# A fused linear-attention and mixture-of-experts kernel: new delays and draws in the order laid out at build time, TensorE by due time, one ones-product for each batch's norm

## The chip, the cores and the metric

The kernel runs on one core of a Trainium2 chip. The metric is the device time of one execution in microseconds. A core has five engines with queues of their own, each worked through in order: TensorE (matrix products, PE in the profile, with its weight loads as PEld), VectorE (DVE), ScalarE (ACT), GpSimd (POOL) and SyncE (SP, which here only issues DMAs). They meet at semaphores. Products land in PSUM, which is eight banks here, called u1, u2, db and ab, two of each; all else lies in SBUF or in DRAM.

## The reference

```python
kv  = einsum('bhsd,bhse->bhde', k, v)            # 8 batches, 8 heads, 576 tokens, 64 wide
o   = einsum('bhsd,bhde->bhse', q, kv)
rms = sqrt(mean(o * o, axis=-1, keepdims=True) + 1e-06)
x   = (o / rms * g_norm) -> (4608, 512)          # tokens by heads*width
p   = domain_probs / (domain_probs.sum(-1) + 1e-09)
for e in range(4):                               # w1[e]: 512x1024, w2[e]: 1024x512
    h = maximum(x @ w1[e], 0)
    out += p[:, e:e+1] * (h @ w2[e])
```

All is float32. The outer loop over experts is 90% and more of the arithmetic.

## The kernel before

**Tiling and steps.** The 4608 tokens are cut into nine chunks of 512: 512 tokens of each of the eight batches, and a ninth chunk with the 64 tokens left of each. The work is 36 steps, step s = 9 e + i, expert e outermost. A step has two parts. `up` makes the hidden layer of a chunk (x w1, then relu), `down` multiplies it with w2, scales it by the probability and adds it to the output, for the first expert by a plain store, for the others by a DMA that adds in DRAM, for the very last step by loading the sum, merging in SBUF and storing. `down` of one step runs beside `up` of the next.

**Fewer products.** Both parts use a scheme with seven products in place of eight, on two levels in `up`: 49 products of 128x128x128 for each of four blocks' worth of work. The operands of the seven are sums and differences of blocks (named 1, 2, 21 or 12, 3 to 7), made on VectorE and GpSimd. In the inner scheme of `up` (lines around 1385 and 1393) and `down_deep` (1707, 1715) ScalarE copies a PSUM bank to another bank as a seed or to SBUF (`snap`), and VectorE adds two of them. `down` has three shapes: seven outer products for each of two token halves, with no inner scheme (the last step); the mixed shape, with outer products 1, 6, 5, 7 plain and 4, 2, 3 by the inner scheme, called from `down` into `down_deep` (steps 0 to 6); and `down_deep` for all seven (steps 7 to 34). One plain product is 16 instructions of 256 columns, one inner product of `up` 8 instructions of 128 columns, one inner product of `down_deep` 16 for a pair of outer forms or 8 for a single one.

**Attention.** `opening` does batch 0 in a way of its own. `attention` does batches 1 to 7, each in the step before the one that needs it, in two halves s of four heads: load q, k, v; transpose q on VectorE (L1023); k times v on TensorE (L1050); q times that (L1075); evacuate four banks, on ScalarE or VectorE (L999, L1000); square on ScalarE (L1099, L1105); sum the squares with a matrix of ones (`total`, L1115 for the 512 tokens, L1121 for the 64 left); root on ScalarE (L1131); inverse and one refining step on VectorE (`invert`, L1137 to L1142); write the 160 columns of 16 partitions to DRAM (`roots`, L1151) and read them back, spread over all partitions (L1158, L1164); scale (L1173, L1180). `x_forms` then makes the seven forms of the chunk and keeps them in DRAM for the later experts.

**The order.** Nothing of the order of instructions is left to run time. Every piece of work is an `Op` given to `Plan.add` with a key (its place in the steps), a cost for each engine that may do it, buffers read and written, and kilobytes if it is a DMA. `Plan.prepare` gives each a due time: the sum of TensorE's costs ahead of its key, then pulled forward along dependencies. `Plan.run` plays the five engines through in time: an engine that is free looks through its pending operations within `REACH` of its first key; SP and TensorE take the first by key that is ready, the others the one with the smallest due time. `ready` says when: after the end of what it depends on plus `CROSS` = 0.2 us, or `SAME` = 0.06 on the same engine; when buffers are free; when one of SP's eight lanes is; and, for operations with `port`, when the port that VectorE and GpSimd share is. `begin` books the times. `deal` adds to the due times of a step a normal draw, whose number for each step is written down in `DEALS`. The order so found is issued as it stands, with waits where the data ask for them. A plan that is wrong about a time thus makes an engine wait on the chip; it doesn't change the order there.

```python
                    best = op
                    if eng in ("PE", "SP"):
                        break
```

Of the kernel before, what the change touches and what calls it, by code (L numbers as in the profile page):

```python
# [42 lines left out]
class Plan:  # L43
# [11 lines left out]
    CROSS, SAME, LANES = 0.2, 0.06, 8  # L55
# [6 lines left out]
    SPREADS = 1.0, 2.0, 4.0  # L62
    DEALS = {
        -2: 25, -1: 39, 0: 49, 1: 28, 2: 72, 3: 8, 5: 18, 6: 22, 7: 12, 8: 22, 9: 17, 10: 9, 11: 22, 12: 28,
        13: 4, 14: 5, 17: 5, 18: 3, 19: 1, 20: 5, 21: 4, 26: 4, 27: 4, 28: 1, 29: 2, 35: 2
# [6 lines left out]
    def add(self, key, cost, fn, reads=(), writes=(), parts=(), kb=0, after=(), port=False, holds=(),  # L72
            early=False, gang=False):
# [3 lines left out]
        op.early, op.gang = early, gang  # L77
# [21 lines left out]
    def prepare(self, slots, later, idle, idle_banks, idle_until):  # L99
# [26 lines left out]
        for op in reversed(self.ops):  # L126
            for d in op.deps:
                cross = self.SAME if op.cost.keys() == d.cost.keys() else self.CROSS
                d.due = min(d.due, op.due - cross - min(d.cost.values()))
# [19 lines left out]
        self.bus, self.port = 3.8, 0.0  # L149
# [10 lines left out]

    def deal(self, step, n):

        draw = random.Random(100 * n + step)
        for op in self.steps[step] + self.steps.get(step + 1, []):
            op.due = op.base + (draw.gauss(0.0, self.SPREADS[n % 3]) if n else 0.0)

# [11 lines left out]
    def save(self):  # L178
        copied = {
            name: {k: type(v)(v) for k, v in getattr(self, name).items()}  # L180
            for name in ("free", "slots", "todo", "waiting", "first")
        }
        copied.update({name: dict(getattr(self, name)) for name in ("live", "ended", "missing", "busy", "written")})
        copied.update({name: list(getattr(self, name)) for name in ("later", "lanes", "wake", "order")})
        copied.update({name: getattr(self, name) for name in ("worked", "bus", "port", "t", "left")})
        return (
            copied, [(o.start, o.end, o.eng) for o in self.ops],
            [(b.left, b.slot, b.ap) for b in self.all_bufs],
        )

    def restore(self, saved):
        copied, ops, bufs = saved
        for name, value in copied.items():
            if isinstance(value, dict):
                value = {k: type(v)(v) if isinstance(v, (dict, list)) else v for k, v in value.items()}
            elif isinstance(value, list):
                value = list(value)
# [177 lines left out]
def kernel(  # L375
# [1194 lines left out]
    def down(s, e, c, mixed=False):  # L1570
# [6 lines left out]
        for t in range(2):  # L1577
# [37 lines left out]
            if mixed:  # L1615
                continue
# [304 lines left out]
```

## Time and profile before

| | |
|---|---|
| median of 3 runs | 1645.11 us (1644.44 to 1647.65) |
| profiled execution | 1645.75 us, span 1644.0 us |
| granted TensorE clock | 1.00 |
| DVE instructions | 2191 |
| DMA | 240.82 MB, 225436 packets |

The span runs from the first to the last instruction of the profiled execution. A matrix product's instructions overlap one another, so the time of a run of them is read from the start of one group to the start of the next, not from a group's busy time. In rows of the timeline the columns are start, length, engine, line, operation, tiles, shape and count, and in brackets the idle time of the engine ahead of it and what ended it. Line 501 is the product of two halves of 64 columns that all parts of the experts use; line 524 is every sum or difference of operands on VectorE and GpSimd; line 530 is every plain load.

### The profile page before, as it was taken

What the parts mean: (1) busy time and instruction counts of PE and PEld (TensorE: products, weight loads), DVE (VectorE), ACT (ScalarE), POOL (GpSimd) and SP (SyncE); (2) the same over time, 40 slices, a digit from 0 to 9 for tenths busy, and PEclk for the clock granted to TensorE, in tenths of its full rate; (3) what the DMA queues carried; (4) which work ended last, traced back from release to release, by engine and by line L of the source; (5) the groups of instructions that cost most, each with busy time, mean ns of one, the idle gap of its engine ahead of it and who ended that gap; (6) DMA issues with size and microseconds to landing.
All of it is one profiled execution on the core that took longest, in us unless ns stands there. A gap on an engine that the chain in (4) does not pass through costs nothing.

```text
span 1644.0 us, 66026 instructions
## 1 busy us (share of the span) xinstructions
PE 1632.1 (99%) x28652; PEld 1551.9 (94%) x28652; DVE 1285.5 (78%) x2191; ACT 972.8 (59%) x2436; POOL 687.0 (42%) x668
## 2 busy tenths in 40 slices
PE   9999999999999999999999999999999999999998
PEld 5588888988999999999999999999999999999996
DVE  5888877788888877877778877777788787677764
ACT  3455554555566666666666666666666566666662
POOL 4232443333433354554354454443455455433331
PEclk9999999999999999999999999999999999999999
DMA  9787786645655435444567454444578444444442
GB/s 237 205 210 185 217 228 174 173 154 187 214 159 152 109 101 149 125 111 111 168 168 162 112 122 111 116 111 115 138 189 184 118 112 117 118 117 106 117 105 52
DMA packets 225436, 240.82 MB, mean 146 GB/s; under 512 B 100954, under 2 KB 165114, under 8 KB 225146
## 3 DMA queue, kind: packets, MB, share of 16 engines
q1 hardware_dynamic: 201594, 199.81, 39.6%
q0 software_dynamic: 23552, 36.78, 14.9%
q8 instruction: 225, 3.69, 0.9%
q14 instruction: 65, 0.53, 0.1%
HBM read 162.21 MB, written 74.33 MB: 144 GB/s over the span
## 4 chain that ended last, share of the span: by engine, by line
PE 97%; DMA 1%; DVE 1%; SPq 0%; issue 0%; ACT 0%; DVEq 0%
PE u L501 48%; PE db L501 31%; PE ab L501 15%; PE ab L1050 1%; DMA kv<-in_v_dram 1%; PE ab L1075 0%; PE ab L1115 0%; DMA big<-in_v_dram 0%; PE db L1075 0%; DMA big<-roots 0%; SPq L530 0%; DVE big L524 0%; DVE big L1173 0%; PE db L902 0%; PE u L863 0%; DMA kv<-in_k_dram 0%
## 5 line engine op out<-in xcount | busy, mean ns | idle before, releaser
L524 DVE TENSOR_TENSOR big<-big,big 128x1024 f32<-128x1024 f32 (+1 forms) x552 | 517.8, 956 | 25.5 <-ACT big L1349 9.8
L501 PE MATMUL u<-xf,big 128*64 128x128 f32 x6496 | 473.6, 273 | 0.0
L501 PE MATMUL db<-big,big 128*64 128x128 f32 (+1 forms) x5328 | 407.5, 292 | 2.0 <-ACT snap L1707 1.2
L501 PE MATMUL u<-xf,w1y 128*64 128x128 f32 x5304 | 396.2, 273 | 0.0
L501 PEld LDWEIGHTS u<-xf,big 128*64 128x64 f32 x6496 | 378.7, 137 | 3.4 <-issue 0.8
L501 PEld LDWEIGHTS db<-big,big 128*64 128x64 f32 x5328 | 316.9, 137 | 29.8 <-ACT snap L1707 1.4
L1393 DVE TENSOR_TENSOR big<-u,snap 128x256 f32<-128x256 f32 x462 | 193.3, 420 | 161.6 <-PE u L501 120.4
L501 PEld LDWEIGHTS u<-xf,w1y 128*64 128x64 f32 x5304 | 310.7, 137 | 3.3 <-issue 1.2
L524 POOL TENSOR_TENSOR big<-big,big 128x256 f32<-128x256 f32 (+1 forms) x169 | 204.4, 1212 | 214.0 <-DVE big L524 89.4
L1385 ACT ACTIVATE snap<-u 128x256 f32<-128x256 f32 x490 | 187.4, 383 | 172.1 <-PE u L501 142.6
L1385 ACT ACTIVATE big<-u 128x256 f32<-128x256 f32 x462 | 175.9, 383 | 76.1 <-PE u L501 52.7
L524 POOL TENSOR_TENSOR big<-big 128x512 f32<-128x512 f32 (+1 forms) x92 | 111.0, 1208 | 161.6 <-DVE big L524 74.5
L1707 ACT ACTIVATE snap<-db 128x256 f32<-128x256 f32 x252 | 89.0, 354 | 128.9 <-PE db L501 116.9
L1349 ACT ACTIVATE big<-big 128x1024 f32<-128x1024 f32 x134 | 140.9, 1051 | 7.8 <-DVE big L524 7.8
L1558 POOL DMA_DIRECT2D out_dram<-big x114 | 99.5, 1122 | 52.2 <-ACT big L1534 43.1
L1715 DVE TENSOR_TENSOR big<-ab,snap 128x256 f32<-128x256 f32 x174 | 73.2, 420 | 59.7 <-ACT snap L1707 39.2
L1385 ACT ACTIVATE u<-u 128x256 f32<-128x256 f32 x245 | 90.8, 371 | 46.9 <-PE u L501 33.3
L524 DVE TENSOR_TENSOR big<-big 128x512 f32<-128x512 f32 (+1 forms) x137 | 102.0, 750 | 1.7 <-POOL big L524 1.1
L1746 POOL TENSOR_TENSOR big<-big 128x512 f32<-128x512 f32 x26 | 33.1, 1274 | 145.9 <-DVE big L524 143.1
L1534 ACT ACTIVATE big<-big,p_all 128x256 f32<-128x256 f32 x190 | 88.8, 500 | 1.8 <-DVE big L1746 1.6
L501 PE MATMUL ab<-kv,big 128*64 128x128 f32 x1296 | 89.8, 273 | 0.0
L501 PE MATMUL ab<-big,big 128*64 128x128 f32 (+1 forms) x1280 | 88.9, 277 | 0.0
(218 smaller groups left out, 2317.2 us busy)
## 6 DMA issues: line engine op xcount, KB each, us to landing
xf<-x SPq DMA_DIRECT2D x104, 512.0 KB, 3.6
xf<-x_h SPq DMA_DIRECT2D x85, 256.0 KB, 3.1
xf<-x SPq DMA_DIRECT2D x78, 256.0 KB, 4.2
out_dram<-big POOLq DMA_DIRECT2D x78, 256.0 KB, 5.9
x<-xf SPq DMA_DIRECT2D x36, 512.0 KB, 3.6
big<-in_moe_w_dram SPq DMA_DIRECT2D x29, 512.0 KB, 6.3
x_h<-big SPq DMA_DIRECT2D x17, 512.0 KB, 3.5
big<-in_moe_w_dram POOLq DMA_DIRECT2D x17, 512.0 KB, 6.1
```

Of the source, the lines that this page charges most:

```text
L501: nc.tensor.matmul(out_[cols], lhsT=lhsT[:, cols], rhs=rhs, **kw)
L524: lambda eng: adder(eng).tensor_tensor(out=out_(), in0=a(), in1=b(), op=op),
L1050: nc.tensor.matmul(bank.ap[o * D:(o + 1) * D, r * D:(r + 1) * D], lhsT=ks[r], rhs=vs[r], start=(j == r == 0), stop=(j == len(sets[0]) - 1) ...
L1349: lambda eng: nc.scalar.activation(out=b.ap[:], in_=b.ap[:], func=ACT.Relu),
L1385: lambda eng: nc.scalar.activation(out=where(), in_=ps.ap[:, 0:HN], func=ACT.Copy),
L1393: lambda eng: nc.vector.tensor_tensor(out=block(whole, a, t), in0=src.ap[:, 0:HN], in1=add_.ap[:], op=ALU.add),
L1534: lambda eng: nc.scalar.activation(out=cell(i, half), in_=ap(), func=ACT.Copy, scale=prob()),
L1558: nc.gpsimd.dma_start(out=dst, in_=cell(i)[parts, :], accum_op=ALU.add)
L1707: lambda eng: nc.scalar.activation(out=where(), in_=group_of(ps.ap), func=ACT.Copy),
L1715: lambda eng: nc.vector.tensor_tensor(out=cell(tq, dq), in0=group_of(src.ap), in1=group_of(add_.ap), op=ALU.add,),
L1746: lambda eng: adder(eng).tensor_tensor(out=whole(to), in0=whole(a), in1=whole(b), op=ALU.add),
```

## The change

It has four parts.

1. The plan's picture of time. One delay across engines becomes several: after TensorE 0.25, to TensorE 0.06, to GpSimd 0.16, on the same engine 0.07, otherwise 0.05, after a landing 0.1, and a buffer is free 0.25 after TensorE or 0.08 after others. An engine may start its next operation before the last ends (`OVERLAP`). The shared port costs -0.14 or 0.1 when it changes hands (`TURN`). The DMAs have a landing time of their own kind, and the rate of the bus is 260 from 45 us on. Some costs of operations change.
2. The choice. TensorE no longer takes the first by key that is ready but the smallest due time, as VectorE, ScalarE and GpSimd do; only SP keeps to the key. The draws are made by a hash, TensorE's with spreads of their own, and `DEALS` has other numbers. To keep the plan legal, the first product of a bank in `up_plain` is named as a dependency of the others.
3. Attention. Evacuations are all on ScalarE. The sums of squares of both halves are one product over 2 x (8 x 4 + 4) calls of 32 columns into one bank of 128 columns, with one root and one inversion for a batch. The result is written in four DMAs (two for each half, 64 partitions, 128 bytes each) and spread as before, the main part now from one run of 1024 values for each half of the partitions.
4. The end. The last two chunks of the last expert change places (8, then 7). The last step uses the mixed shape, with forms 4, 2, 3 ahead in key order, the plain 1, 6, 5, 7 behind, no dependency between the two, banks u1 for its second and third sums, and stores after the plain ones. Of the last expert's inner w2 operands only those of 1, 6, 5, 7 get a buffer apart.

```diff
-    CROSS, SAME, LANES = 0.2, 0.06, 8
+    LANES = 8
+    AFTER_PE, TO_PE, TO_POOL, SAME, OTHER, LANDED, FREED = 0.25, 0.06, 0.16, 0.07, 0.05, 0.1, 0.08
+    OVERLAP = {"PE": 0.0, "DVE": 0.085, "ACT": 0.105, "POOL": 0.05, "SP": 0.0}
+    TURN = {"DVE": -0.14, "POOL": 0.1}
...
+    SPREADS_PE = 0.0, 0.5, 1.5
+    RATE, OPEN = 260.0, 45.0
+    FIRST = "SP",
     DEALS = {
...
     def deal(self, step, n):
 
-        draw = random.Random(100 * n + step)
+        k = len(self.SPREADS)
+        wide = self.SPREADS[n % k] if n else 0.0
+        wide_pe = self.SPREADS_PE[n // k % len(self.SPREADS_PE)] if n else 0.0
         for op in self.steps[step] + self.steps.get(step + 1, []):
-            op.due = op.base + (draw.gauss(0.0, self.SPREADS[n % 3]) if n else 0.0)
+            z = wide_pe if "PE" in op.cost else wide
+            op.due = op.base + (z * self.noise(n, step, op.n) if z else 0.0)
...
+    def delay(self, d, eng):
+
+        if d.kb:
+            return self.LANDED
+        if d.eng == "PE":
+            return 0.0 if eng == "PE" else self.AFTER_PE
+        if d.eng == eng:
+            return self.SAME
+        return {"PE": self.TO_PE, "POOL": self.TO_POOL}.get(eng, self.OTHER)
...
-            when = max(when, d.end + (self.SAME if d.eng == eng else self.CROSS))
+            when = max(when, d.end + self.delay(d, eng))
...
-            when = max(when, self.port)
+            when = max(when, self.port + (0.0 if eng == self.held else self.TURN[eng]))
...
-                    if eng in ("PE", "SP"):
+                    if eng in self.FIRST:
                         break
...
-            self.bus = max(self.bus, t + 1.5) + op.kb / 215.0
+            self.bus = max(self.bus, t + 1.5) + op.kb / (215.0 if t < self.OPEN else self.RATE)
             op.end = self.bus + 0.5
+            if t >= self.OPEN:
+                op.end = max(op.end, t + op.lands)
             self.lanes = self.lanes[1:] + [op.end]
         else:
-            op.end = self.busy[eng] = t + op.cost[eng]
+            op.end = t + op.cost[eng]
+            self.busy[eng] = op.end - self.OVERLAP[eng]
             if op.kb:
-                op.end += 9.0 if op.kb == 512 else 8.0
+                op.end += op.lands
...
-    sides = const.tile([P, 48], F32, name="sides")
-    ones = [sides[:, 16:48], sides[:, 0:32]]
+    sides = const.tile([P, 60], F32, name="sides")
+    ones = [sides[:, 28 - 4 * i:60 - 4 * i] for i in range(8)]
...
-            def total(eng, ss=ss, xh=xh, s=s):
-                for o in range(2):
+        when = at(3.7)
+        ss, wide, both = Buf("ab", f"ss{b}"), 4 * R, x_halves(b)
+
+        def total(eng):
+            for s in range(2):
+                for i in range(8):
                     for j in range(NR):
                         nc.tensor.matmul(
-                            ss.ap[j * R:(j + 1) * R, 0:P], lhsT=ones[o],
-                            rhs=xh.ap[:, (2 * j + o) * P:(2 * j + o + 1) * P],
-                            start=(o == 0), stop=(o == 1), skip_group_check=True,
+                            ss.ap[j * R:(j + 1) * R, 2 * s * R:(2 * s + 1) * R], lhsT=ones[i],
+                            rhs=both[s].ap[:, (8 * j + i) * R:(8 * j + i + 1) * R],
+                            start=(s == i == 0), stop=(i == 7), skip_group_check=True,
                         )
                 for j in range(NR):
                     nc.tensor.matmul(
-                        ss.ap[j * R:(j + 1) * R, P:P + GR], lhsT=ones[0],
-                        rhs=xs.ap[:, s * P + j * GR:s * P + (j + 1) * GR],
+                        ss.ap[j * R:(j + 1) * R, (2 * s + 1) * R:(2 * s + 2) * R], lhsT=ones[0],
+                        rhs=xs.ap[:, s * P + j * R:s * P + (j + 1) * R],
                         start=False, stop=True, skip_group_check=True,
                     )
 
-            plan.add(
-                when, {"PE": 0.75}, total, reads=[xh, xs], writes=[ss]).wide = {ss: P + GR}
+        plan.add(
+            when, {"PE": 1.27}, total, reads=both + [xs], writes=[ss]).wide = {ss: wide}
...
+            for to, src, at_ in (
+                (sent, main[:].rearrange("r (n t) -> n r t", t=R), 2 * s * R),
+                (sent_left, rest_at[:], (2 * s + 1) * R),
+            ):
+                plan.add(
+                    when, SPC,
+                    lambda eng, to=src, at_=at_: nc.sync.dma_start(
+                        out=to, in_=both[0].ap[0:P:2, at_:at_ + R]),
+                    reads=both[:1], writes=[to], kb=8, lands=2.6,
+                )
...
+        ends = s == E * NCH - 1
         order = [m for m in MERGED if not (mixed and m in (2, 4, 3))]
+        if ends:
+            down_deep(s, e, c, ((4, 2), (3,)), base - 0.1, h, merge, send, True)
+            base += 3 / 7
...
-                    after=(second[-1:] if m in (1, 5) else []) + firsts[t:t + 1],
+                    after=(second[-1:] if m in (1, 5) and not ends else []) + firsts[t:t + 1],
...
+    CHUNKS[E - 1][-2:] = NCH - 1, NCH - 2
...
-                down(s, e, c, s < NCH - 2)
+                down(s, e, c, True)
```

231 lines of the change are left out of this document (117 added, 114 removed).

## The prediction

> **What bounds the kernel now.** I read the page first, then the stages, the waits of TensorE, and the timeline at the places where it waits.
>
> ```profile
> span 1644.0 us, 66026 instructions
> PE 1632.1 (99%) x28652; PEld 1551.9 (94%) x28652; DVE 1285.5 (78%) x2191; ACT 972.8 (59%) x2436; POOL 687.0 (42%) x668
> PE 97%; DMA 1%; DVE 1%; SPq 0%; issue 0%; ACT 0%; DVEq 0%
> ```
>
> TensorE is busy for 99% of the span and is 97% of the chain that ended last. The next view cuts the span into stages (busy time of TensorE, of its weight loads, of VectorE, ScalarE and GpSimd, then granted clock and DMA).
>
> ```profile
> 0.00:20.00 20.00, 17.53 (x354) 14.71 (x356) 6.65 (x24) 9.63 (x28) 4.77 (x15) 1.00 0.90 298
> ...
> 840.00:1240.00 400.00, 400.00 (x7334) 400.00 (x7332) 319.95 (x510) 252.39 (x636) 185.16 (x179) 1.00 0.53 133
> 1600.00:1644.00 44.00, 39.10 (x494) 30.47 (x490) 21.99 (x36) 12.85 (x30) 4.78 (x5) 1.00 0.27 49
> ```
>
> The middle, 840 to 1240 us, has no idle time at full clock: an order of the same products can't be shorter there, only longer. Idle time lies in the opening, at the end, and in a few single waits between. The waits of TensorE (total, times, longest):
>
> ```profile
> PE ab L1866 <- POOL ident masks.py:199: 1.4, 1, 1.4
> PE db L501 <- ACT snap L1707: 1.2, 1, 1.2
> PE u L501 <- DVE big L1173: 0.9, 1, 0.9
> PE ab L922 <- DVE big L797: 0.7, 1, 0.7
> PE ab L1050 <- DMA kv<-in_v_dram: 0.6, 1, 0.6
> PE db L501 <- DVE big L1715: 0.6, 1, 0.6
> PE u L501 <- DVE big L1393: 0.5, 1, 0.5
> PE db L501 <- ACT small L1000: 0.5, 1, 0.5
> PE u L863 <- DMA big<-in_v_dram: 0.4, 1, 0.4
> PE db L501 <- ACT big L1707: 0.4, 1, 0.4
> ```
>
> The first, 1.4, is the identity at the start, which the change leaves alone. The other nine are 5.8 us. This is all that a better order can win: 0.35% of the time.
>
> **Term 1, the last step.** `down` for the last step now goes the mixed way: 8 large products (four forms, two token halves) instead of 14, and three forms by the deep route.
>
> ```profile
> 1600.57 1.04 PE L501 MATMUL db<-big,big 128*64 128x128 f32 x16
> 1601.44 0.61 PE L501 MATMUL u<-xf,w1y 128*64 128x128 f32 x8
> ...
> 1635.86 1.90 PE L501 MATMUL u<-big,big 128*64 128x256 f32 x16
> 1637.58 1.90 PE L501 MATMUL ab<-big,big 128*64 128x256 f32 x16
> 1639.53 0.48 DVE L1542 SCALAR_TENSOR_TENSOR big<-ab,p_all,big 128x256 f32<-128x256 f32 x1 [1.24 <-PE ab L501]
> ```
>
> From start to start, a large product takes 1637.58 - 1635.86 = 1.72 us, a deep pair (16 instructions of 128 columns) 1601.44 - 1600.57 = 0.87, a deep single half of it, 0.44. Removed: 6 x 1.72 = 10.3. Added: 7 pairs and 7 singles, 7 x 0.87 + 7 x 0.44 = 9.2. Net -1.1 us, on TensorE's own path. The added subtractions that make the deep operands lie on VectorE, which sits idle for 1.24 us ahead of each merge there. While a deep form isn't ready, the large products, whose link to the deep ones is cut for this step, can fill in; if they don't, one wait such as the 0.4 above comes back. Bounds -1.1 to -0.1.
>
> Behind the last product stood one merge (0.48) and a result of chunk 8 in two stores; now stand two merges, since form 7 serves two cells, and one store, since the last chunk is now 7. An issue takes about half a us (next fence: 8 issues in 4.66), so +0.48 - 0.5 is zero, bounds -0.5 to +0.5. The saved issue is the cover of the second merge; without it the tail grows by 0.5.
>
> **Term 2, the ones-product.** Two runs of 16 instructions of 128 columns and 8 of 32 become one run of 144 instructions of 32 columns for a batch (2 halves x 36 calls x 2).
>
> ```profile
> 49.05 0.64 PE L1115 MATMUL ab<-big,sides 128*32 128x128 f32 x16
> 49.51 0.24 PE L1121 MATMUL ab<-snap,sides 128*32 128x32 f32 x8
> 49.68 3.65 PE L501 MATMUL u<-big,big 128*64 128x512 f32 x16
> ...
> L1121 PE MATMUL ab<-snap,sides 128*32 128x32 f32 x112 | 3.4, 194 | 0.0
> ```
>
> Now: 49.68 - 49.05 = 0.63 for a half, 1.26 for a batch. The 8 short ones cover 0.24 us and each lasts 0.194, so 8 starts lie within 0.046: 6.6 ns apart, as they go to four groups of 32 columns in turn. 144 x 6.6 ns = 0.95, and some 0.15 to enter and leave (0.63 less four groups of 0.109 and two of 0.027; 0.109 is a quarter of 0.44): 1.10. Seven batches: 7 x (1.10 - 1.26) = -1.1. The other end: if each costs what it does in the group's row, 3.4/112 = 30 ns, a batch takes 4.4 and seven lose 22. I take -1.0; the row within one run is the nearest.
>
> A rule speaks against this. The Trainium skill, "TensorE: Matmul & The Clock Gate", section "Wait — 56ns, not 53.3ns?", gives a floor of about 25 ns from start to start however few columns stream; by it, as an estimate, 144 would take 3.6 us. The 6.6 ns measured above is below that floor, so here it can hold for a group of four at most (4 x 6.6 = 26 ns).
>
> VectorE and ScalarE are also relieved or loaded, none of it on the end path but through the stalls:
>
> ```profile
> L1137 DVE RECIPROCAL big<-big 128x160 f32<-128x160 f32 x14 | 16.1, 1147 | 4.5 <-ACT big L1131 4.4
> L999 DVE COPY small<-ab 128x320 f32<-128x320 f32 x11 | 5.2, 483 | 1.2 <-PE ab L1075 1.2
> L999 DVE COPY small<-db 128x256 f32<-128x256 f32 x12 | 4.8, 417 | 2.1 <-PE db L1075 2.1
> ```
>
> Fourteen reciprocals of 160 columns become seven of 128: 16.1 - 7 x 1.147 x 0.8 = 9.7 us less, and the three products behind each (0.33) fall likewise, some 8 us. The 23 copies on VectorE (10.0 us) all go to ScalarE, which has 40% of its time free. Cover gone, the copies cost ScalarE 10 us more within 40 to 360 us.
>
> **Term 3, the stalls that are there.** The chain of batch 1's norm shows how the order makes them.
>
> ```profile
> 56.70 0.29 ACT L1105 ACTIVATE snap<-small 128x128 f32<-128x128 f32 x1
> ...
> 59.92 3.62 PE L501 MATMUL db<-big,big 128*64 128x256 f32 x32
> ...
> 63.91 0.64 PE L1115 MATMUL ab<-big,sides 128*32 128x128 f32 x16
> ...
> 67.57 0.65 SPq L1151 DMA_DIRECT2D roots<-big  x1
> 68.27 4.66 SPq L530 DMA_DIRECT2D small<-in_q_dram  x6
> 73.04 1.29 SPq L1158 DMA_DIRECT2D big<-roots  x2
> ...
> 78.22 1.28 DVE L1173 SCALAR_TENSOR_TENSOR big<-small,gcol,big 128x1024 f32<-128x1024 f32 x1 [0.29 <-DMA big<-roots]
> 79.56 0.66 PE L501 MATMUL u<-big,big 128*64 128x128 f32 x8 [0.92 <-DVE big L1173]
> ```
>
> The squares are done at 57.0, but the ones-product starts at 63.91: large products whose place in the key order is earlier go first, though they are due later. By due time it could start some 6.9 us sooner. Against that, the joint norm is longer for a first half and for the queue of SP: four writes of roots instead of one ahead of the spreads (+3 x 0.65 = 2.0), a second spread (+1.3), a second scale (+1.28), less a shorter inversion (-0.4): +4.2 us. Net up to 2.7 earlier, and the wait of 0.92 goes.
>
> Each new delay can be held against rows shown: VectorE's end 79.50 to TensorE's start 79.56 is 0.06 (the plan of before reckons 0.2, the new one 0.06); TensorE's next start after the ones-product 49.68 to ScalarE's root below is 0.23 (0.2 and 0.25); VectorE's operations of 0.42 start 0.33 apart (0.42 and 0.335).
>
> ```profile
> 49.91 0.39 ACT L1131 ACTIVATE big<-ab,eps 128x160 f32<-128x160 f32 x1 [0.47 <-PE ab L1121]
> ...
> 46.67 0.42 DVE L524 TENSOR_TENSOR w1y<-w1y,big 128x256 f32<-128x256 f32 x1
> 47.00 0.42 DVE L524 TENSOR_TENSOR w2y<-big 128x256 f32<-128x256 f32 x1
> ```
>
> So the new plan sees these waits as the chip does and can order around them. The two waits for loads in the opening (0.4, and 0.7 at L922 behind the first batch) are paced by DMA at a 0.90 share; of the rest I take about three quarters: -3.5 of 5.8. Bounds 0 to -5.8.
>
> **Term 4, new stalls.** The old plan counts VectorE a quarter too long and the way to TensorE 0.14 too long, and so leaves air ahead of most products; the new one takes that air out, and may start a product 0.06 after its operand. Where the chip is later than planned, TensorE waits, and all behind it. What is unmodelled: VectorE's operations of 128x1024 took 1.28 us above (L1173), and 2.13 below, where GpSimd works beside it. I take two waits of 0.4: +0.8; bounds 0 to +17 (first rival below).
>
> ```profile
> 118.40 2.13 DVE L524 TENSOR_TENSOR big<-big,big 128x1024 f32<-128x1024 f32 x1
> ```
>
> Sum: -1.1 + 0 - 1.0 - 3.5 + 0.8 = -4.8 us. The profiled execution took 1645.75 us (1644.0 and 1.75 around it), so 1640.95; the median of the runs shown is 1645.11, 0.64 below, so **1640.3 us**.
>
> **The rivals.**
> Slower, air gone: TensorE by due time takes products whose operand has only just come, all along the steps from 440 to 1600 us, where it now never waits. For it: the zero slack of that stage, VectorE at 80%, and the spread of 1.28 to 2.13. Against it: products of two steps (`up` and `down`) are in reach at any time, so one that is ready long since is mostly there, and due times favour old ones. At 0.6 us each (mean of the nine above) and one for each of the 28 steps that is +17: 1640.3 - 0.8 + 17 = 1656.5. It decides from 14 such waits on, one in every second step (8.2 us, 4.9 of gain and 3.3).
> No change: the stalls move rather than go, as the queues of ScalarE and SP are still in order and the opening is paced by DMA; what is left is the certain part, -1.1 and some of term 2: 1643.5. In this case the order doesn't do what it says. For it: each of the nine occurs once and has another line or releaser, so no one fault makes them all. Against: most follow a chain through ScalarE or VectorE, where the old delays are wrong.
> The joint norm is late: if the 6.9 us of head start isn't used, the 4.2 falls on TensorE in the first two steps, where it already waits for L1173: +8.4, less the other gains, 1640.3 + 8.4 = 1648.7.
> The ones-product at 30 ns an instruction: +22 + 1 = 1663.
>
> **How the numbers follow.** A measurement of this kernel tells 0.2%, 3.3 us, from no change. Forecast 0.48, no change 0.27, air gone 0.16, joint norm late 0.06, ones-product 0.03. The forecast's own range is 1636.5 (all 5.8 won, no new wait, term 1 and 2 full, and half a us at the tail) to 1641.8. The whole range reaches up over no change and the late norm to 1651, where some eight or more new waits beyond that are left out. Faster: the forecast, 0.48. Same: no change and half of the late norm, 0.30. Slower: 0.22.
>
> **What would show it.** Right: the last fourteen large products are eight, and TensorE's last start is some 5 us earlier; 144 instructions in about 1.1 us in each of seven runs; the wait for L1173 gone, with the ones-product right behind the squares; 440 to 1600 us still without idle time. Wrong: TensorE's waits sum to more than 5.8, above all many small ones beside L1385, L1393 and L1707; or the ones-product above 1.3 us.

## The result, and the profile after

| | before | after |
|---|---|---|
| median | 1644.78 us (1643.45 to 1647.65, 6 runs) | 1652.2 us (1648.63 to 1654.36, 6 runs) |
| profiled execution | 1645.75 us, span 1644.0 | 1650.71 us, span 1648.9 |

The changed kernel is slower: ratio 1.004, 95% interval 1.0024 to 1.0057. The forecast was 1640.3, the range ended at 1651.0. One run of land9, below, took 1878.35 us at a granted clock of 0.85 and is left out of its median and range. The page of after, then its stages (columns as in the prediction: stretch, its length, busy time of TensorE, its weight loads, VectorE, ScalarE, GpSimd, then granted clock, DMA share, GB/s):

```profile
span 1648.9 us, 67550 instructions
PE 1634.0 (99%) x29396; PEld 1557.3 (94%) x29396; DVE 1322.4 (80%) x2212; ACT 974.1 (59%) x2462; POOL 603.0 (37%) x617
q8 instruction: 231, 3.78, 0.9%
PE 95%; DMA 2%; issue 1%; DVE 1%; SPq 1%; ACT 0%; POOL 0%; DVEq 0%; POOLq 0%; ACTq 0%
```

```profile
0.00:40.00 40.00, 37.48 (x494) 25.12 (x496) 16.55 (x48) 14.87 (x41) 17.56 (x27) 0.96 1.03 236
40.00:360.00 320.00, 314.82 (x5710) 261.90 (x5708) 244.39 (x449) 173.82 (x440) 80.79 (x90) 1.00 0.71 194
...
840.00:920.00 80.00, 77.28 (x1408) 76.56 (x1406) 69.30 (x127) 50.45 (x127) 35.96 (x38) 1.00 0.68 163
...
17.00:20.40 3.40, 3.40 (x43) 2.84 (x42) 2.23 (x8) 1.44 (x5) 1.45 (x2) 0.51 1.12 161
```

The same view of before:

```profile
0.00:40.00 40.00, 37.53 (x506) 23.71 (x508) 20.06 (x52) 16.30 (x46) 16.42 (x26) 1.00 0.92 236
40.00:360.00 320.00, 315.47 (x5080) 263.04 (x5078) 261.20 (x483) 170.20 (x421) 111.89 (x107) 1.00 0.71 196
```

Three stages lose. From 0 to 40 the idle time is as before, but for 3.4 us the granted clock was 0.51, which is worth 3.4 x 0.49 = 1.7 us of full clock. That is 0.001 of the time. The mean granted clock was 0.999 in three of the six runs of after (1648.63 to 1650.71 us) and 0.998 in the other three (1653.68 to 1654.36), so none of the six ran at the full clock throughout. From 40 to 360 TensorE is idle 5.18 us instead of 4.53, though this is the stage in which the change wanted to win. From 840 to 920, where before had no idle time, it is idle for 2.72. The waits of TensorE in after (total, times, longest) say what for:

```profile
PE db L521 <- ACT ab L1749: 2.0, 1, 2.0
PE ab L1139 <- issue: 1.7, 1, 1.7
...
PE u L521 <- DVE big L1429: 0.9, 1, 0.9
PE db L521 <- issue: 0.9, 1, 0.9
PE db L924 <- DVE big L819: 0.8, 2, 0.5
PE u L521 <- ACT snap L1421: 0.6, 1, 0.6
PE db L521 <- ACT big L1570: 0.6, 1, 0.6
PE u L521 <- issue: 0.4, 1, 0.4
```

In this numbering of lines 521 is the product of the experts (501 before), 1139 and 1145 are the ones-product, 1421, 1429 and 1749 the copies and sums of the inner scheme, 1570 scales a result by its probability, 819 and 924 belong to the opening; in some of the kernels below the same lines stand one higher or lower. Two kinds are new. "Issue" has no releaser: no semaphore, no DMA, no engine. The timeline shows where two of the seven runs of the ones-product stand, one with such a wait and one without:

```profile
147.44 0.73 PE L1139 MATMUL ab<-big,sides 128*32 128x32 f32 x62
...
150.50 0.23 PE L1139 MATMUL ab<-big,sides 128*32 128x32 f32 x4 [1.73 <-issue]
...
150.75 0.66 PE L521 MATMUL u<-small,w1y 128*64 128x128 f32 x8
...
249.01 0.73 PE L1139 MATMUL ab<-big,sides 128*32 128x32 f32 x62
...
250.40 0.44 PE L521 MATMUL db<-big,big 128*64 128x256 f32 x2
```

The undisturbed run takes 250.40 - 249.01 = 1.39 us; six of the seven take 1.36 to 1.39, and the one at 147.44 takes 3.31. A start follows a start by (0.73 - 0.20) / 61 = 8.7 ns, 0.20 being the length of one. The seven together are 11.6 us against 14 x 0.635 and 0.2 = 9.1 in before, and 1.3 us more of "issue" lie behind two of them (0.9 at 112.16, 3.5 us behind a run's end, and 0.4 at 253.16, 2.8 behind).

What these waits have in common can be counted in the traces. The instruction queue of the page moved 231 packets of 16 KB, and TensorE has 59130 instructions (products, weight loads, a few on semaphores): 256 to a packet. Counted from the start of the program, 3521 instructions lie ahead of the start at 112.16, 4801 ahead of that at 150.50 and 8641 ahead of that at 253.16. All three counts are 193 more than a multiple of 256, so the waits lie whole blocks of 256 instructions apart. The last packet of that queue ahead of each of them landed at 110.80, 148.92 and 251.70, which is 1.4, 1.6 and 1.5 us before the wait ended. The same holds for every wait without a releaser in all the traces of this case, 20 in eight kernels: ahead of each the count is 193 above a multiple of 256, and each ends 1.3 to 1.6 us after such a packet landed. TensorE has used up a block of instructions and waits for the next.

The other new kind is ScalarE's copy of weights, line 617, whose operand is loaded by a DMA that adds in DRAM (line 623). The rows of GpSimd, ScalarE and TensorE in time:

```profile
859.14 1.97 POOL L623 DMA_DIRECT2D big<-in_moe_w_dram  x1
870.38 1.06 ACT L617 ACTIVATE small<-big 128x1024 f32<-128x1024 f32 x1 [3.02 <-DMA big<-in_moe_w_dram]
871.73 1.31 POOL L623 DMA_DIRECT2D small<-in_moe_w_dram  x1 [3.73 <-ACT big L1749]
879.39 1.06 ACT L617 ACTIVATE big<-small 128x1024 f32<-128x1024 f32 x1 [2.50 <-DMA small<-in_moe_w_dram]
880.62 0.38 ACT L1749 ACTIVATE ab<-db 128x256 f32<-128x256 f32 x1
881.05 0.66 PE L521 MATMUL db<-w2y,big 128*64 128x128 f32 x8 [1.97 <-ACT ab L1749]
```

The load issued at 859.14 landed 11.2 us later, the one of 871.73 after 7.6. The new plan reckons 6.0 (`lands`), the old one 9.0. ScalarE's queue is in order, so the evacuation of line 1749 stands behind the copy, and TensorE behind that.

### The profile page after: what moved, and what is told of

Its sections match the earlier page's. It is cut to its first block, busy times and chain, and to the rows that moved or that the text cites. A ratio compares the mean times of both kernels' runs of the same rounds, so it can differ in the third digit from the quotient of the medians.

```text
span 1648.9 us, 67550 instructions
## 1 busy us (share of the span) xinstructions
PE 1634.0 (99%) x29396; PEld 1557.3 (94%) x29396; DVE 1322.4 (80%) x2212; ACT 974.1 (59%) x2462; POOL 603.0 (37%) x617
## 4 chain that ended last, share of the span: by engine, by line
PE 95%; DMA 2%; issue 1%; DVE 1%; SPq 1%; ACT 0%; POOL 0%; DVEq 0%; POOLq 0%; ACTq 0%
PE u L521 46%; PE db L521 30%; PE ab L521 15%; PE ab L1072 1%; PE ab L1097 1%; PE ab L1139 1%; DMA xf<-x_h 0%; DMA big<-in_moe_w_dram 0%; DMA small<-in_moe_w_dram 0%; DMA kv<-in_k_dram 0%; PE db L1097 0%; DMA big<-roots 0%; PE u L885 0%; PE ab L1910 0%; DVE big L544 0%
## 5 line engine op out<-in xcount | busy, mean ns | idle before, releaser
L544 DVE TENSOR_TENSOR big<-big,big 128x256 f32<-128x256 f32 (+1 forms) x535 | 494.1, 939 | 30.9 <-ACT big L1385 14.3
L521 PE MATMUL u<-xf,big 128*64 128x128 f32 x6784 | 493.3, 273 | 1.1 <-ACT snap L1421 0.6
L521 PE MATMUL db<-big,big 128*64 128x128 f32 (+1 forms) x5608 | 431.6, 290 | 1.9 <-issue 0.9
L521 PEld LDWEIGHTS u<-xf,big 128*64 128x64 f32 x6784 | 397.4, 137 | 4.4 <-issue 1.7
L521 PEld LDWEIGHTS db<-big,big 128*64 128x64 f32 x5608 | 335.7, 137 | 30.4 <-issue 2.6
L1429 DVE TENSOR_TENSOR big<-u,snap 128x256 f32<-128x256 f32 x436 | 183.2, 421 | 117.9 <-PE u L521 80.6
L544 POOL TENSOR_TENSOR big<-big,big 128x256 f32<-128x256 f32 (+1 forms) x146 | 151.9, 1042 | 232.2 <-DVE big L544 111.1
L1421 ACT ACTIVATE big<-u 128x256 f32<-128x256 f32 x436 | 166.3, 383 | 81.2 <-PE u L521 61.6
L1749 ACT ACTIVATE snap<-db 128x256 f32<-128x256 f32 (+1 forms) x256 | 90.2, 352 | 109.3 <-PE db L521 88.7
L1788 POOL TENSOR_TENSOR big<-big 128x512 f32<-128x512 f32 x19 | 24.2, 1274 | 164.8 <-DVE big L544 135.1
```

The source lines that it names most:

```text
L521: nc.tensor.matmul(out_[cols], lhsT=lhsT[:, cols], rhs=rhs, **kw)
L544: lambda eng: adder(eng).tensor_tensor(out=out_(), in0=a(), in1=b(), op=op),
L1421: lambda eng: nc.scalar.activation(out=where(), in_=ps.ap[:, 0:HN], func=ACT.Copy),
L1429: lambda eng: nc.vector.tensor_tensor(out=block(whole, a, t), in0=src.ap[:, 0:HN], in1=add_.ap[:], op=ALU.add),
L1749: lambda eng: nc.scalar.activation(out=where(), in_=group_of(ps.ap), func=ACT.Copy),
L1788: lambda eng: adder(eng).tensor_tensor(out=whole(to), in0=whole(a), in1=whole(b), op=ALU.add),
```

## The experiments

Each is named by its label. All have 5 to 12 timed runs beside the kernel before on the same chip.

**fill.** Eight products with the identity put into the opening's waits, to keep the clock up.

```diff
+                    for _ in range(fill.get((name, met[name]), 0)):
+                        idle(next(b for b in turn[0].outs if b.kind == "ab").ap)
```

> The changed kernel with its order as it is, and 8 short products of the identity, four matmuls each, put into TensorE's queue in the opening where it waits in the profile after (at 14.4, 16.5, 18.2 and 24.3 us). Theory 'clock': the opening's waits let the granted clock fall for one or two stretches of 3.41 us, and this, not the waits, is most of the loss and of the spread: all executions at clock 1.000, the median 4 to 7 us below the changed kernel's 1652.2 (its executions at 0.999 took 1648.6 to 1650.7, those at 0.998 took 1653.7 to 1654.4), so 1645 to 1648, and the spread under 3 us. Rival 'the waits themselves': the clock comes up but the time falls by no more than the 1.7 us of work that a half clock holds up in one stretch: 1650 or more. Rival 'not the gaps': the clock falls as before, 1652.

Measured: 1651.03 us (1649.52 to 1654.87), ratio 1.0039 (1.0027 to 1.0051). The clock was 1.00, the first ones-product came 0.7 us sooner (55.49 us against 56.19), and the time is that of after: the theory "clock" missed, the rival "the waits themselves" came out. Its waits:

```profile
PE u L521 <- issue: 2.6, 2, 1.6
PE ab L1139 <- issue: 2.4, 2, 1.5
```

Four of its five runs have a mean clock of 1.000, and the median is only 1.2 us below that of after: most of the lost time is elsewhere. The eight products also moved the blocks of 256 by 128 instructions, and the waits without a releaser stand at other places than in after and are 5.2 us instead of 3.0.

**ones48.** The ones-product of the changed kernel as 48 instructions of mostly 128 columns in the same order.

```diff
-                for i in range(8):
+                for o in range(2):
...
-                            rhs=both[s].ap[:, (8 * j + i) * R:(8 * j + i + 1) * R],
+                            rhs=both[s].ap[:, (2 * j + o) * P:(2 * j + o + 1) * P],
```

> The changed kernel with its order as it is; the ones-product of a batch is 48 instructions, 32 of them 128 columns wide, in place of 144 of 32 columns, written over the same 128 columns of the bank, so the norms computed are not the reference's. Theory 'instruction feed': the three idle stretches of TensorE of 1.9, 1.0 and 0.5 us that the profile after ends by 'issue', one within and two behind a ones-product, come from 288 instructions taken in 1.2 us; they go, and each of the seven runs takes 1.27 in place of 1.39: 3.5 + 0.8 = 4.3 us less. Rival 'chance': the stretches come from something else that loads instructions late (DMA load); they stay, and only 0.8 goes. Read in the trace, since the clock's spread hides some of it in the times.

Measured: 1644.11 us (1641.45 to 1646.15), ratio 0.9994 (0.9985 to 1.0002). No wait over 0.2 us without a releaser is left, each run takes 1.135 us, and the median is 8.1 us below that of after. Part of this can be the clock, which was 0.999 or 1.000 in its runs; against fill, whose clock was as high, it is 6.9 us. The largest waits that are left:

```profile
PE ab L1910 <- POOL ident masks.py:199: 1.4, 1, 1.4
PE u L521 <- DVE big L1429: 1.4, 3, 0.8
PE db L924 <- DVE big L819: 0.8, 2, 0.5
```

The norms of this kernel are not those of the reference, so it shows a time and is no version to use.

**ones80.** The same, with 80 instructions: 64 columns for the main part, the norms being those of the reference; the root and the inversion then work on 192 columns instead of 128.

```diff
-                for i in range(8):
+                for i in range(4):
...
-                            rhs=both[s].ap[:, (8 * j + i) * R:(8 * j + i + 1) * R],
+                            rhs=both[s].ap[:, (4 * j + i) * 2 * R:(4 * j + i + 1) * 2 * R],
```

> The changed kernel with its order as it is; the ones-product of a batch is 80 instructions, 64 columns wide for the main part, with the norms the same; root and inversion then run over 192 columns in place of 128 (some 0.65 us of VectorE more for a batch). Theory 'instruction feed': about as with 48 instructions, the idle stretches ended by 'issue' gone or below 0.5 us in sum, a run at 1.2 to 1.3 us, 3.5 to 4.5 us less. Rival 'chance': they stay. If the number of instructions matters in steps, one of the three stretches is left.

Measured: 1647.41 us (1643.76 to 1650.15), ratio 1.0014 (1.0005 to 1.0023). Again no such wait, 1.155 us a run, 4.8 us below after. What is left above before isn't the ones-product: TensorE waits 2.0 us for line 1422, 1.6 of it behind a late landing, and 1.7 in five waits for VectorE; two of these, 0.4 and 0.3, stand behind the inversion, which now takes 2.6 us instead of 2.0.

**land9.** The accumulating load reckoned to land after 9.0 us, all else as changed.

```diff
-            reads=[to], writes=writes, kb=512, lands=6.0,
+            reads=[to], writes=writes, kb=512, lands=9.0,
```

> The changed kernel with one figure of the plan put back: a weight load that adds in DRAM is reckoned to land 9.0 us after its issue in place of 6.0 (in the trace after it took 5.3 to 11.2). The order is the same up to the first such load at some 430 us and another from there on. Theory 'landing': TensorE's waits between 800 and 900 us, 3.2 us in the trace after, behind ScalarE's copy that waits for such a load, go; 440 to 1600 us has under 1 us of idle time; 3 us less than the changed kernel. Rival 'a draw': any other order from there on has waits of its own, between 1 and 5 us, at other places.

Measured: 1651.06 us (1647.26 to 1653.05, six runs), ratio 1.0032 (1.002 to 1.0043). The stage is mended:

```profile
840.00:920.00 80.00, 80.00 (x1470) 80.00 (x1468) 68.80 (x126) 52.26 (x130) 43.83 (x40) 1.00 0.72 167
```

The span of its trace is 3.4 us shorter than that of after, with a stretch of low clock (0.52 for 3.4 us) in both. The median is 1.1 us lower where 3 was expected, which can't be told from nothing, as the runs scatter by 6 us. Two waits without a releaser (1.7 and 0.4) remain, at the same counts of instructions, 4801 and 3521, as in after, whose order it shares up to some 430 us.

**before_fine.** The converse of ones48: the kernel before, its order untouched, with each product of 128 columns of the norm cut into four of 32.

```diff
+                    for t in range(0, P, GR):
...
-                            ss.ap[j * R:(j + 1) * R, 0:P], lhsT=ones[o],
+                                ss.ap[j * R:(j + 1) * R, t:t + GR], lhsT=ones[o],
```

> The kernel before, its order untouched, with each 128-column product of the norm cut into four of 32 columns: 72 instructions a half instead of 24, the same columns in all. Instruction feed: the half then issues 144 instructions (72 weight loads, 72 products) in about 0.65 us, half of what a batch's run issues after the change, and the halves stand 15 to 30 us apart. If the supply of instructions runs dry within a burst, one or more waits of 0.5 to 2 us without a releaser show beside the norm's products, of which before has none, and the time rises by 1 to 4 us, to 1646 to 1649. Rate alone: the half takes 72 times 8.3 ns, 0.60 to 0.70 us as in the kernel before (0.635), no wait beside it, and the time stays within 1 us of 1644.8; then it is the burst of 288 in one stretch that drains the supply, not the small products as such.

Measured: 1645.93 us (1644.66 to 1647.64), ratio 1.0007 (0.9998 to 1.0016), 1.0 us above the 1644.91 of its runs of before. One of the fourteen halves was interrupted, the others were not:

```profile
103.72 0.68 PE L1117 MATMUL ab<-big,sides 128*32 128x32 f32 x55
104.74 0.27 PE L1117 MATMUL ab<-big,sides 128*32 128x32 f32 x9 [0.34 <-issue]
```

The wait is again at the end of a block of 256. An undisturbed half takes 0.76 us instead of 0.635, more than the 0.60 to 0.70 of "rate alone", 14 x 0.12 = 1.7 us in all. So 72 short products in a stretch cost little, and twice as many cost more. Neither expectation is met in full: there is a wait beside the norm, but one in fourteen halves, and smaller than the 0.5 to 2 us of the instruction feed.

**before_end.** The kernel before with the change's last step alone.

```diff
+        if ends:
+            down_deep(s, e, c, ((4, 2), (3,)), base - 0.1, h, merge, send, True)
...
+    CHUNKS[E - 1][-2:] = NCH - 1, NCH - 2
```

> The kernel before with the change's last step alone (last two pieces of the last step in swapped order, its second products mixed with the first ones); the timing of the plan, the norm and the landing stay. The prediction's term 1 gave -1.1 us for the step and 0 for the tail; the comparison of the two traces gave about -1.2 of work and -0.3 of tail. If that holds, 1643.0 to 1644.0 and the last fourteen large products become eight; if the gain was eaten (the order of the plan shifts before the last step), 1644.5 to 1646.

Measured: 1644.59 us (1643.41 to 1648.56), ratio 0.9999 (0.999 to 1.0007), 0.3 below its runs of before. In the traces the last step is 0.8 us shorter than in before (the span is 2.1 us shorter, but 1.3 of that was won ahead of it, where the order is the same). Part of the gain is eaten by two waits in the new last step, which the order of before wasn't laid out for:

```profile
1625.28 0.66 PE L501 MATMUL db<-big,small 128*64 128x128 f32 x8 [0.57 <-ACT snap L1711]
...
1628.09 0.66 PE L501 MATMUL db<-kv,small 128*64 128x128 f32 x8 [0.41 <-ACT u L1711]
```

**best.** ones80 with its costs in the plan as measured, the accumulating load at 9.0, and the order searched again.

```diff
-            when, {"PE": 1.27}, total, reads=both + [xs], writes=[ss]).wide = {ss: wide}
+            when, {"PE": 1.16}, total, reads=both + [xs], writes=[ss]).wide = {ss: cols}
...
-            when, {"DVE": 0.62 + 0.0113 * wide}, invert, reads=[ss, both[0]], writes=both[:1], port=True)
+            when, {"DVE": 2.65}, invert, reads=[ss, both[0]], writes=both[:1], port=True)
```

> The kernel after the change with three costs of its plan set to what the traces measured (the norm's products 1.16 us as 80 instructions, its inversion 2.65 us over 192 columns, an accumulating load landing after 9.0 us in place of 6.0) and the order searched again, to a plan of 1633.2 us against 1631.6 of the kernel after and 1641.5 of the kernel before. If the loss came from the feed of instructions and from the two mispriced items, the plan is kept better: no wait without releaser, no wait for an accumulating load, 1637 to 1643 us. If a plan without air is slower on the chip whatever its prices (each small delay is paid at once), 1645 to 1650, with the waits small and many.

Measured: 1647.8 us (1645.53 to 1654.4), ratio 1.0025 (1.0015 to 1.0035). Neither expectation fits: the time is that of the second, but the waits are few and large, and one without a releaser is there, 1.0 us at 13.12 in the opening, at the end of a block as well. The largest, by engine in time:

```profile
602.02 0.52 SPq L550 DMA_DIRECT2D xf<-x_h  x1
...
609.86 0.69 DVE L544 TENSOR_TENSOR xf<-xf,xf 128x512 f32<-128x512 f32 x1 [3.61 <-DMA xf<-x_h]
...
612.41 0.66 PE L521 MATMUL ab<-small,big 128*64 128x128 f32 x8 [2.57 <-DVE big L1758]
```

Another transfer, another place, the same mechanism: a load for which the plan reckons 4.0 us took 7.8. The plan's landing times stand near the middle of each kind's spread (an `xf<-x` load in after: median 3.6, upper tenth above 6.0, longest 8.6; a store that adds into the output, reckoned 5.6: median 5.7, upper tenth above 8.0), and a transfer that is later than the middle is as common as one that isn't.

**best_open.** best, and in the opening the readers of a pair's scores are issued after both products of the pair.

```diff
+        order[first + 1:other + 1] = [
+            o for o in order[first + 1:other] if o not in between] + [order[other]] + between
```

> The same as best, and in the opening the readers of a pair's raw scores are issued after both of its products rather than between them, so that the second product doesn't wait for the first one's reader of the same bank of PSUM. If those waits (0.5 to 0.7 us each at 14.4, 16.5 and 24.3 us after the change) cost what they show, 1 to 2 us faster than best; if VectorE and ScalarE come late in their turn, the same or up to 1 us slower.

Measured: 1651.72 us (1647.58 to 1652.61), ratio 1.0033 (1.0021 to 1.0045). The waits moved from the first products (1.1 us in sum for VectorE and ScalarE) to the next ones (0.6 and 0.6); nothing was won. That the median is 3.9 us above that of best was not expected, and its trace, 0.3 us longer than best's, doesn't explain it; all its runs have a mean clock of 0.997 to 0.999.

**tail, tail_b, best_c.** tail reckons each kind of landing near its upper tenth; tail_b is the same with another order from the search; best_c is best with another order.

```diff
-    def load(key, buf, dst, src, kb, reads=(), also=(), lands=4.0, issue=0.55):
+    def load(key, buf, dst, src, kb, reads=(), also=(), lands=6.2, issue=0.55):
...
-            reads=[to], writes=writes, kb=512, lands=9.0,
+            reads=[to], writes=writes, kb=512, lands=9.5,
...
-                lands=5.6 if e and not again else 4.5,
+                lands=8.0 if e and not again else 5.4,
```

> As best, but each kind of transfer is reckoned to land after a time near the upper tenth of what the traces show rather than near the middle (an x load 6.2 us in place of 4.0, weights 8.0 in place of 6.0, an output sum 8.0 in place of 5.6, and so on), and the order searched again: its plan is 1634.0 us, 0.8 longer than best's 1633.2. If late landings are what an order without air pays for (best's waits of 2.6 us at 612 and 1.5 us at 1205 both go back to a transfer that landed late), no wait over 0.5 us is left between 440 and 1600 us, the runs scatter less than the 9 us of best, and the median is 1640 to 1644. If the loss is not in the landings but in the opening and the norm's stretch (0 to 360 us), the time stays at 1645 to 1649.

> The same reckoning as tail with another order from the same search, of 1637.4 us in the plan. Late landings: again no wait over 0.5 us between 440 and 1600 us and a scatter as narrow as tail's; the time is tail's plus up to 3.4 us, the difference of the plans, 1642 to 1647. Luck of one order: waits of 1 us and more behind late transfers come back in it.

> The reckoning of best (transfers land at the middle of what the traces show) with another order from the search, 1633.6 us in the plan, 0.4 shorter than tail's. Late landings: waits behind transfers at other places than in best, 2 to 5 us in sum after 440 us, and 1645 to 1650. Luck of one order: as fast as tail.

| | runs | median us (range) | ratio (95%) |
|---|---|---|---|
| tail | 10 | 1642.08 (1640.54 to 1643.98) | 0.9979 (0.997 to 0.9988) |
| tail_b | 11 | 1646.33 (1643.88 to 1648.14) | 1.0004 (0.9995 to 1.0013) |
| best_c | 11 | 1644.64 (1642.82 to 1646.76) | 0.9993 (0.9984 to 1.0002) |

tail is faster than both kernels: 0.2% below before, 10 us below after. The stages, first best and best_c:

```profile
360.00:1600.00 1240.00, 1235.54 (x22492) 1229.45 (x22490) 1027.20 (x1658) 765.59 (x1932) 520.25 (x494) 1.00 0.52 134
```

```profile
360.00:1600.00 1240.00, 1238.91 (x22554) 1232.78 (x22552) 1036.45 (x1661) 765.27 (x1938) 515.54 (x493) 1.00 0.53 134
```

then tail, and last tail_b:

```profile
40.00:360.00 320.00, 318.26 (x5382) 266.77 (x5380) 246.36 (x446) 176.63 (x443) 91.98 (x90) 1.00 0.74 200
360.00:1600.00 1240.00, 1239.73 (x22578) 1234.21 (x22575) 1034.32 (x1654) 767.72 (x1939) 510.26 (x498) 1.00 0.52 134
```

```profile
40.00:360.00 320.00, 315.46 (x5281) 261.39 (x5278) 244.84 (x445) 173.95 (x437) 89.45 (x87) 1.00 0.74 195
360.00:1600.00 1240.00, 1239.69 (x22572) 1233.80 (x22570) 1035.32 (x1654) 767.47 (x1939) 523.37 (x500) 1.00 0.53 135
```

Between 360 and 1600 us TensorE is idle 4.5 and 1.1 us with landings at the middle, 0.3 and 0.3 with landings at the upper tenth. That is what late landings predict, though best_c's 1.1 is below the 2 to 5 that were expected. The medians show a second thing: one reckoning gives orders 3 to 4 us apart. tail_b's plan is itself 3.4 us longer than tail's, and their traces part before 360 us (idle 1.7 in tail, 4.5 in tail_b, which also has a stretch of low clock in the opening). The plans of best and best_c are 0.4 us apart, their medians 3.2, and their traces part in the middle. tail's whole gain over best is therefore not the landings' alone.

**tail144.** tail's order to the instruction, with the 144 short products back.

```diff
-                for i in range(4):
+                for i in range(8):
...
-                            rhs=both[s].ap[:, (4 * j + i) * 2 * R:(4 * j + i + 1) * 2 * R],
+                            rhs=both[s].ap[:, (8 * j + i) * R:(8 * j + i + 1) * R],
```

> The order of tail, kept to the instruction, with the 144 short products of the changed kernel put back in place of the 80. Rate and feed: each of the seven runs takes 1.36 to 1.39 us in place of 1.155, 1.6 us in sum, and waits without a releaser of 0.5 to 2 us show in or right behind some of them, 2 to 4 us in sum; the median rises from 1642.1 by 3.5 to 5.5 us, to 1645.5 to 1647.5. Rate alone: 1.6 us, 1643 to 1644, and no such wait. If the order absorbs it (the norm's stretch has waits that end on other engines), 1641.5 to 1643.

Measured: 1650.96 us (1647.95 to 1653.74), ratio 1.0039 (1.0026 to 1.0053): 8.9 us above tail, more than expected. The order is tail's; what differs is the shape of one product, and with it the width of the root and the inversion (128 columns instead of 192) and the writes of the norm. The clock is the same in both, 0.999 in the mean of the runs. Its waits, and its run at 149.11 in the timeline:

```profile
PE ab L1145 <- issue: 2.3, 2, 1.7
PE ab L1139 <- issue: 2.0, 2, 1.4
...
PE u L521 <- issue: 1.2, 1, 1.2
```

```profile
149.11 0.73 PE L1139 MATMUL ab<-big,sides 128*32 128x32 f32 x62
...
152.20 0.26 PE L1145 MATMUL ab<-snap,sides 128*32 128x32 f32 x5 [1.68 <-issue]
152.39 0.66 PE L521 MATMUL u<-small,w1y 128*64 128x128 f32 x8
```

The same run in tail:

```profile
145.35 0.65 PE L1140 MATMUL ab<-big,sides 128*32 128x64 f32 x32
...
146.50 0.66 PE L521 MATMUL u<-small,w1y 128*64 128x128 f32 x8
```

3.28 us against 1.15. The sum of the waits without a releaser is 5.5 us; four of the seven runs are interrupted, after 68 to 139 of their 144 products, and the fifth wait, 1.2 us, is 4.3 us behind a run. With 7 x (1.39 - 1.155) = 1.6 us for the runs themselves that is 7.1 of the 7.3 us between the two spans. In tail none is interrupted.

## Why the prediction was wrong

Its sum said -4.8 us for the span; the trace has +4.9. The medians are 7.4 us apart; the profiled execution was one of the three faster ones of after, and no trace shows the others.

| | predicted | measured in the trace |
|---|---|---|
| Term 1, last step and tail | -1.1 + 0 | about -1.4 |
| Term 2, ones-product | -1.0 | +3.8 (2.5 in the runs, 1.3 of issue behind them) |
| Term 3, stalls that were there | -3.5 | -2.7 (5.8 to 3.1) |
| Term 4, new stalls | +0.8 | 2.8 of late landings, 1.7 of clock, and 0.7 in gaps too small to list: +5.2 |

**The step that failed is Term 2.** It took 6.6 ns from start to start out of eight instructions, and 144 x 6.6 + 0.15 = 1.10 us; a whole run shows 8.7 ns and 1.36 to 1.39. That alone turns -1.0 into 7 x 1.39 - 9.1 = +0.6. The rest is a cost that the prediction had no term and no rival for: 144 products and 144 weight loads use up a whole block of 256 instructions in as little as 1.1 us, and the next block isn't there yet. ones48, ones80 and tail144 show it, each with the order held: the waits without a releaser come and go with the number of instructions in the stretch, and with them 5 to 9 us (4.8 in ones80, 8.1 in ones48, 8.9 in tail144). The upper bound, 30 ns an instruction, was not it either: an undisturbed run is far from 4.4 us. The floor of about 25 ns that the Trainium skill gives (the section cited in the prediction) does not hold for a single one of these products; a round of four, 4 x 8.7 = 35 ns, lies above it.

That it is the fetch of instructions follows from where the waits stand: all 20 at the first instruction of a block, all 1.3 to 1.6 us after a packet landed, in kernels with 144, 80 and 72 products alike. The packets ahead of them took no longer than others (0.9 to 1.6 us; the median of all is 1.0), so it isn't a DMA that was late. How fast a block is used up decides. Seven blocks in all the traces lasted under 2 us, and each was followed by such a wait, of 0.57 to 1.75 us; of 33 that lasted 2 to 4.3 us eight were, of 3137 longer ones five. The shortest block of before lasts 5.2 us, of ones48 4.8, of tail 3.9. It is also why seven equal runs of 288 instructions differ: only where a block begins near the start of a run is the whole block short. The Trainium skill, "Runtime: NRT & Kernel Launch", section "Instruction fetch mechanics", has such blocks too (16 KiB, 256 instructions) and says that their fetch is mostly hidden; by it, one run of 288 uses up more than a block. The packets agree; with 5.5 us of waits in tail144, hidden does not hold for this stretch.

**Term 4** had the right sign and not the mechanism. It looked for the plan's error in the durations of VectorE and the delays between engines. The error that counted was in the landings: the change replaced 9.0 for the accumulating load by 6.0 and gave all others a time near their middle. The prediction read `lands` in the diff and priced it at nothing. Its bounds (0 to +17) held. The rival "air gone" put this in many waits of 0.6 all along the steps; there were three between 360 and 1600 us, the longest 2.0, so it was right that the air protects and wrong about from what. The low clock is no matter of this one execution: none of the six runs of after had a mean of 1.000, and the traces of land9 (0.52 for 3.4 us), best_open (0.52) and tail_b (0.60) have such a stretch too; the prediction had no term for it. fill, almost free of it, took nearly the same time, so it is not most of the loss.

**Term 3** was about right. In after, 2.0 us of stalls on VectorE and ScalarE are left from 40 to 360 us and 1.1 in the opening; the wait for line 1173 shrank from 0.9 to 0.3. The opening did not improve, which the prediction had left out of its three quarters.

**Term 1** was right in size where the order is laid out for the step (1.1 of work by its count of products; from the start of the last group of products to the end 1648.9 - 1642.77 = 6.1 us against 1644.0 - 1637.58 = 6.4); without that (before_end) the last step gains 0.8 in the trace, and the 0.3 of the medians lies within their noise. The tail came out 0.3 shorter and not at zero: the prediction took half a us for an issue from "8 issues in 4.66", but that row has 6, so 0.78 each, and 0.48 - 0.78 = -0.3.

The joint norm wasn't late, and the middle stayed without idle time but for the landings, as "what would show it" asked. It named "the ones-product above 1.3 us" as a sign of being wrong, and that sign came; so did waits above 5.8 us in sum (8.9 without the identity's), but few and large ones, not many small ones.

Open stays: why best and best_c, from one reckoning and with plans of nearly one length, differ by 3.2 us; what lets the granted clock fall in one execution and not in another; and the opening's waits, 1.1 us in after and in tail alike, which best_open only moved.

## What to carry to other kernels

Price a burst of very short instructions by the number of instructions in the stretch, weight loads counted, and not by their columns: the same sums as 80 products instead of 144 were worth 4.8 and 8.9 us. On TensorE look at the time in which any 256 instructions in a row are used up: under 2 us a wait followed each time here, above 4.3 us almost never. In an order laid out at build time, give each transfer the landing time of its late tenth; here that made the plan 0.8 us longer and left 0.3 us of idle time in the long middle in place of 1.1 and 4.5. A gain that the plan itself reports is a statement about its costs: from before to after its length fell by 9.9 us and the chip's time rose by 7.4.

## What was not expected of the hardware

TensorE can wait 1.7 us for its own instructions inside a run of independent products: they come in blocks of 256, and all 20 waits without a releaser stand at the start of a block, 1.3 to 1.6 us after a packet of 16 KB landed. The granted clock fell to between 0.51 and 0.60 for 3.4 us in the opening of four of the profiled executions (after, land9, best_open, tail_b) and stayed at 1.00 there in others of nearly the same order (ones48, ones80). Two loads of one kind, 13 us apart, landed after 11.2 and 7.6 us.
